# Hourglass attention into a quick-GELU MoE: scores on 64 partitions from batch 2 on, and a re-ordered start

## The chip, the cores and the metric

The kernel runs on one core of one Trainium2 chip. The metric is the device time of the whole kernel in microseconds, the median of several runs; lower is better. The engines have these short names in the profile: PE (TensorE matmul), PEld (TensorE weight load), DVE (VectorE), ACT (ScalarE), POOL (GpSimd, here "Pool") and SP (SyncE, which here only issues DMAs). PSUM is the memory that TensorE writes; SBUF holds everything else.

## The reference

Attention over 8 batches, 8 heads, 576 tokens and a head size of 64, in two parts that are added: a local part, in which each token sees the tokens less than 4 away, and a part in which q, k and v are first averaged over groups of 4 tokens (144 groups) and the result is repeated 4 times. The sum, 4608 tokens by 512, goes through a feed-forward layer of width 2048.

```python
    q_d = q.reshape(B, H, Sd, factor, D).mean(axis=3)        # k_d, v_d alike
    out_d = sm_attn(q_d, k_d, v_d)
    out_up = np.repeat(out_d, factor, axis=2)
    mask = np.abs(pos[:, None] - pos[None, :]) < factor
    scores = np.where(mask, scale * np.matmul(q, k.transpose(0, 1, 3, 2)), -1e9)
    out_local = np.matmul(softmax(scores), v)
    x = out_up + out_local                                   # to 4608 x 512
    h = x @ w_in
    return (h * (1.0 / (1.0 + np.exp(-1.702 * h)))) @ w_out
```

## The kernel before

The order of instructions on each engine is the order in which the code is written; no scheduler moves them. The feed-forward part runs in 9 groups of 512 tokens (the loop from L800). In a group, `mm1` makes 16 blocks of 4 matmuls (L616) into the two PSUM banks `PM`, each followed by the activation on ACT (L627), and `mm2` makes 4 output tiles of 16 matmuls (L672), which ACT scales (L657) and SP stores (L662). Group g carries the attention of batch b = g + 1 with it: `attention` returns seven steps, and `POS` (L701) says ahead of which block or matmul each is put (group 0: `POS_0`). With `POS`, steps 13 (`s_pe(0)`: scores of heads 0 to 3), 16 (`s_act(0)`: exp and mask) and 33 (`s1`: both for heads 4 to 7), 42 and 53 (`avn`: probabilities times v, for pairs of heads 0, 1 and then 2, 3), 62 and 71 (`tr`: transposing back and writing x). A number of 16 or more stands in `mm2`, at that number less 16.

Ahead of the blocks of a group stands the preparation of its batch (L818 to L831):

- `prep_qk` (L266) lets DVE transpose k and q of 4 heads (L260). A head's 64 dimensions come to lie as 32 partitions times a pair `a` of neighbouring elements, so the four heads fill the 128 partitions.
- `pool_qk` (L270) adds 4 tokens to one on Pool, in two additions (L276, L285), into `kdT` and `qdT`.
- `load_qk` issues four loads of the next batch's k and q on Pool's queue (L194); `prep_v` (L289) casts v on Pool; `load_v` (L214) issues ten loads of the next batch's v on SP; `prep_v4` (L293) adds 4 tokens of `v4` to one in six additions on Pool (L297, L300) into `vd`. `load_v4` (L223) loads `v4` with six DMAs on SP, for b over 2 at the start of the batch's own group, behind the last store of the group before.

`scores` (L340) multiplies in tiles of 32 rows by 64 columns: 5 blocks of tokens, two halves `a`, two sides `par` and four heads make 80 matmuls (L351), the two halves accumulating. `scores_d` (L362) does the same with the averaged q and k, 24 matmuls (L369). `av_local` (L402, matmuls at L408) and `av_down` (L416, L430) multiply with v; `av_down` is the first reader of `vd`, in three parts, one for each third of the 144 groups. `normalise` divides on DVE (L441, L443), `transp` and `merge` (L449, L546) bring x into `xT`.

PSUM is three double banks `PA` for attention and two banks `PM` for the feed-forward part.

The start, ahead of the loop (L710 to L794), does batch 0's attention alone. Loads wait at two gates, which are tiny copies that read one tile and write another, so that the load behind must wait: w_in's gate at L728 (Pool waits for a piece of v 0), and v 1's load, whose gate L708 is a copy on DVE that waits for w_out's first load. w_out's second half waits on Pool (L808) for v 1. Batch 0's averaged scores of heads 4 to 7 go into `PA[1]` (L757), between the first and the second pair of heads; their exp on ACT frees that bank for the second pair. `turned` (L776) transposes a pair of heads and copies the result to `xT` (`copy_x`, four copies on ACT); `part` starts the first feed-forward blocks as the pieces of x come.

Of the kernel before, what the change touches and what calls it, by code (L numbers as in the profile page):

```python
# [8 lines left out]
FP32 = mybir.dt.float32  # L9
BF16 = mybir.dt.bfloat16  # L10
AF = mybir.ActivationFunctionType
ALU = mybir.AluOpType
# [7 lines left out]
def kernel(  # L20
# [18 lines left out]
    inv_sqrt_d = 1.0 / math.sqrt(D)  # L39
    KSTART = (0, 56)  # L40
    QSTART = (0, 60)

    ctx.enter_context(
        tc.manual_schedule(engines={ET.PE, ET.Activation, ET.DVE, ET.Pool, ET.SP})
# [19 lines left out]
    eds = [persist.tile([128, 2, 464], BF16, name=f"ed{i}") for i in range(2)]  # L64
    v4 = persist.tile([128, 3, HP, 4 * D], FP32, name="v4")
    kdT = [persist.tile([128, 160, 2], BF16, name=f"kdT{i}") for i in range(NQ)]

    PA = [psum.tile([128, 2, 512], FP32, name=f"pa{i}") for i in range(3)]
    PM = [psum.tile([128, 512], FP32, name=f"pm{i}") for i in range(2)]
# [51 lines left out]
    def fill():  # L121
        nc.vector.memset(wz, 0.0)
        for t in kdT:
            nc.vector.memset(t[:, SD:160, :], 0.0)
        for t in vbs:
            nc.vector.memset(t[:, :, :, 64:65], 1.0)
        for t in vds:
            nc.vector.memset(t[:, :, :, 64:65], 4.0)
        for t in es:
            nc.vector.memset(t[:, :, 300:304], 1.0)  # L130
        for t in eds:
            nc.vector.memset(t[:, :, 432:464], 1.0)
# [122 lines left out]

    def prep_1(name, b, qd):
        store, dst = {"k": (kf, kT), "q": (qf, qT)}[name]
        tt = work.tile([128, S, 2], BF16, name=f"{name}T{qd}", tag=f"{name}T{qd}", bufs=1)
        t32 = tt.rearrange("p t a -> p (t a)").bitcast(FP32)
        nc.vector.transpose(  # L260
            out=t32.rearrange("p (i c) -> p c i", c=18),
            in_=store[b, qd].bitcast(FP32).rearrange("p (c d) -> p c d", c=18),
        )
        dst[b, qd] = tt

    def prep_qk(b, qd):  # L266
        prep_1("k", b, qd)
# [2 lines left out]
    def pool_qk(b, qd, names="kq"):  # L270
        for name, src in (("k", kT), ("q", qT)):
            if name not in names:
                continue
            sv = src[b, qd].rearrange("p (j f) a -> p j f a", f=4)
            t1 = work.tile([128, SD, 2, 2], FP32, name="pq", tag="pq")
            nc.gpsimd.tensor_tensor(  # L276
                out=t1, in0=sv[:, :, 0:2, :], in1=sv[:, :, 2:4, :], op=ALU.add
            )
            if name == "k":
                dst = kdT[qd][:, 0:SD, :]  # L280
            else:
                t = work.tile([128, SD, 2], BF16, name=f"qdT{qd}", tag=f"qdT{qd}", bufs=1)
                qdT[b, qd] = t
                dst = t
            nc.gpsimd.tensor_tensor(  # L285
                out=dst, in0=t1[:, :, 0, :], in1=t1[:, :, 1, :], op=ALU.add
            )
# [51 lines left out]

    def scores(b, qd, barred=False):  # L340
        sp = [ps_tile(), ps_tile()]
        if barred:
            bar_others(sp)
        for i in range(5):
# [16 lines left out]

    def scores_d(b, qd, sd=None):  # L362
        sd = sd or ps_tile()
        for kc in range(3):
            for a in range(2):
                for r in range(4):
                    rows = slice(32 * r, 32 * r + 32)
                    j = r % 2
                    nc.tensor.matmul(  # L369
                        sd[64 * j : 64 * j + 64, r // 2, SD * kc : SD * kc + SD],  # L370
                        lhsT=kdT[qd][rows, 48 * kc : 48 * kc + 64, a],
                        rhs=qdT[b, qd][rows, :, a],
                        start=(a == 0), stop=(a == 1),
# [143 lines left out]
    def copy_x(b, hp, x):  # L517
        t0 = b * S
        for par in range(2):
            nc.scalar.copy(  # L520
                out=sub(xT[hp], t0 + 3 + 57 * par, (114, 5), (1, 57)),
                in_=sub(x[par], 3 - 3 * par, (57, 5), (1, 57)),
            )
            nc.scalar.copy(
                out=sub(xT[hp], t0 + 573 * par, (1, 3)),
                in_=sub(x[par], 285 * par, (1, 3)),
            )
# [173 lines left out]
    POS = [13, 16, 33, 42, 53, 62, 71]  # L701
    POS_0 = [16, 18, 27, 54, 68, 60, 76]
    VDP_0 = 52

    o, y, x = {}, {}, {}

# [18 lines left out]
    sp = scores(0, 0, barred=True)  # L725
    exp_local(0, sp)
    prep_qk(0, 1)
    nc.gpsimd.tensor_copy(out=w_in_bf[0:1, 0, 0:1], in_=vf[0][0:1, 1, 0, 0:1])  # L728
    load_w_in(0, 512)
    pool_qk(0, 1)  # L730
    load_w_in(512, 512)
    load_w_in(1024, 1024)
    for qd in range(NQ):
# [16 lines left out]
        prep_v(0, nc.vector, i=slice(i, i + 1))  # L750
    warm(6)
    prep_vd_pe(0, PA[2])
    o[0] = PA[0]
    av_local(0, 0, o[0])
    av_down(0, 0, o[0])
    y[0] = normalise(o[0])
    sd = scores_d(0, 1, PA[1])  # L757
    exp_down(1, sd)
    nc.scalar.preload_act_table_set("silu_and_others")
    for hp in range(1, 3):  # L760
        o[hp] = PA[hp]
        av_local(0, hp, o[hp])
        av_down(0, hp, o[hp])
        y[hp] = normalise(o[hp])
    warm(1)

    gT0 = new_gT()
    acc = PM + [PA[n][:, u, :] for n in (1, 2, 0) for u in range(2)]
# [31 lines left out]
    for g in range(n_groups):  # L800
# [15 lines left out]
                load_qk(2, qd)  # L816
            loads_2()
        elif b < B:  # L818
            if b > 2:
                load_v4(b)  # L820
            prep_qk(b, 0)
            pool_qk(b, 0)
            if b + 1 < B:
                for qd in range(NQ):
                    load_qk(b + 1, qd)
            prep_v(b, nc.gpsimd)
            if b + 1 < B:
                load_v(b + 1)
            prep_qk(b, 1)
            pool_qk(b, 1)  # L830
            prep_v4(b, nc.gpsimd)  # L831
        steps = {}
        if b < B:
            for n, f in zip(POS if g else POS_0, attention(b, None if g else (1, 2))):
                steps.setdefault(n, []).append(f)
            if g == 0:
                steps.setdefault(VDP_0, []).append(lambda: prep_vd_pe(1, PA[2]))
        gT = new_gT() if g else gT0
# [32 lines left out]
```

The softmax here doesn't subtract the row's maximum and nothing guards it: scores larger than these inputs give would overflow.

## Time and profile before

| What | us |
|---|---|
| median of 11 runs | 333.92 (331.88 to 335.98) |
| the profiled execution, its own time | 333.1 |
| span of that execution in the profile | 331.3 |
| L616, 528 matmuls of `mm1` into PM: busy | 120.2 |
| L672, 493 matmuls of `mm2` into PM: busy | 114.1 |
| L351, 1280 matmuls of `scores`: busy | 14.0 |
| L369, 384 matmuls of `scores_d`: busy | 9.7 |
| L260, 32 transposes on DVE, 1.24 to 1.25 each: busy | 39.9 |
| L276 and L285, 64 additions on Pool: busy | 58.4 |
| L297 and L300, 36 additions on Pool: busy | 36.5 |
| Pool's idle time that a transpose of k ended | 104.4 |

Times are of one execution, counted from the span's start. A matmul's busy time is that of all matmuls of the line together, since they overlap; the mean of a single one (some 200 ns for the small ones) is longer than its share. A line of the timeline gives start, length, engine, code line, what is written from what, and in brackets the idle time before it with what ended it. The chain of waits is followed back from the last instruction: at each moment it names the work that the end waited for, and "issue" is time for which the profile shows no reason. SPq is time in which SP issues a DMA. The DMA share of a window is the mean busy share of 16 DMA engines and can go a little over 1, as packets overlap.

### The profile page before, as it was taken

The numbers are of one execution on the slowest core, as the hardware profiler recorded it, in microseconds if no ns is written. First come the engines' busy times: TensorE is split into PE (matmuls) and PEld (weight loads), VectorE is DVE, ScalarE is ACT, GpSimd is POOL, SyncE is SP. The second block draws the span as 40 slices with busy tenths as digits, with TensorE's granted clock in tenths as the row PEclk, the third lists the DMA queues.
The fourth block names the chain that finished last, engine by engine and source line by source line (L and its number), as shares of the span: only waits on it lengthen the run. The fifth ranks groups of instructions, "written<-read, shape, count | busy, mean of one in ns | idle before, by whom it ended". The sixth has DMA issues, their size and how long they took to land.

```text
span 331.3 us, 11215 instructions
## 1 busy us (share of the span) xinstructions
PE 309.1 (93%) x4986; PEld 159.5 (48%) x5043; DVE 132.1 (40%) x213; ACT 184.5 (56%) x323; POOL 138.3 (42%) x168
## 2 busy tenths in 40 slices
PE   8657999889999999999999999998999999999995
PEld 3445455545554455445544554445444544444444
DVE  4757302690367127712672167316740570000000
ACT  2543585366836774667467745675466647425611
POOL 7791734029802990199019900991099000000000
PEclk9977999999999999999999999999999999999999
DMA  7999979999913992299329921993180110011011
GB/s 126 184 177 211 180 139 189 192 230 199 190 55 100 205 199 76 89 190 192 108 75 211 205 90 67 203 197 102 45 176 2 44 57 32 2 64 63 2 60 66
DMA packets 63552, 41.36 MB, mean 125 GB/s; under 512 B 44048, under 2 KB 54416, under 8 KB 63504
## 3 DMA queue, kind: packets, MB, share of 16 engines
q1 hardware_dynamic: 55056, 26.95, 35.1%
q0 software_dynamic: 8304, 13.63, 23.6%
q8 instruction: 39, 0.64, 0.9%
q14 instruction: 9, 0.07, 0.1%
q10 hardware_dynamic: 144, 0.07, 0.1%
HBM read 44.83 MB, written 9.44 MB: 164 GB/s over the span
## 4 chain that ended last, share of the span: by engine, by line
PE 87%; issue 4%; SPq 3%; DVE 2%; DMA 2%; ACT 1%; DVEq 0%; ACTq 0%
PE pm L616 35%; PE pm L672 33%; SPq L214 3%; PE pa L351 3%; PE pa L616 2%; PE pa L430 2%; PE pa L408 2%; PE pa L369 2%; PE pa L457 2%; DMA vf<-in_v_dram 2%; PE pa L672 1%; PE pm L687 1%; DVE y L443 1%; PE pa L483 1%; ACT vd L321 0%
## 5 line engine op out<-in xcount | busy, mean ns | idle before, releaser
L616 PE MATMUL pm<-xT,w_in_bf 128*128 128x512 bf16 x528 | 120.2, 380 | 1.2 <-DVE xT L559 0.5
L672 PE MATMUL pm<-w_out_bf,gT 128*128 128x512 bf16 x493 | 114.1, 379 | 5.4 <-issue 5.2
L627 ACT ACTIVATE gT<-pm 128x512 bf16<-128x512 f32 x136 | 81.0, 598 | 44.6 <-PE pm L616 44.6
L616 PEld LDWEIGHTS <-w_in_bf 128*128 128x128 bf16 x576 | 55.8, 98 | 68.0 <-issue 2.0
L672 PEld LDWEIGHTS <-gT 128*128 128x128 bf16 x560 | 51.8, 98 | 59.5 <-issue 0.2
L276 POOL TENSOR_TENSOR pq<-kT 128x576 f32<-128x576 bf16 x16 | 18.6, 1160 | 104.4 <-DVE kT L260 104.4
L394 DVE TENSOR_TENSOR es<-es,mask 128x600 bf16<-128x600 bf16 x28 | 20.5, 750 | 94.7 <-ACT es L380 94.0
L657 ACT ACTIVATE osb<-pm 128x512 f32<-128x512 f32 (+2 forms) x35 | 20.8, 594 | 40.2 <-PE pm L672 35.9
L532 ACT COPY od<-pa 128x384 f32<-128x384 f32 (+1 forms) x56 | 18.4, 412 | 30.8 <-DVE y L443 22.4
L443 DVE TENSOR_TENSOR y<-pa,rc 128x896 bf16<-128x896 f32 x32 | 34.9, 1092 | 1.1
L553 DVE TENSOR_TENSOR xT<-pa,od 128x570 bf16<-128x570 f32 x28 | 21.1, 754 | 10.4 <-ACT od L532 10.3
L380 ACT ACTIVATE es<-pa 128x600 bf16<-128x600 f32 x32 | 19.8, 668 | 7.4 <-PE pa L351 7.1
L297 POOL TENSOR_TENSOR v<-v 112x512 f32<-112x512 f32 x18 | 22.8, 1264 | 0.0
L659 DVE TENSOR_SCALAR osb<-pm 128x128 f32<-128x128 f32 x1 | 0.3, 292 | 55.3 <-ACT osb L657 55.3
L260 DVE STREAM_TRANSPOSE kT<-kb 128x576 f32<-128x576 f32 x16 | 20.0, 1251 | 3.9 <-DMA kb<-in_k_dram 3.8
L260 DVE STREAM_TRANSPOSE qT<-qb 128x576 f32<-128x576 f32 x16 | 19.9, 1242 | 1.6 <-DMA qb<-in_q_dram 1.5
L276 POOL TENSOR_TENSOR pq<-qT 128x576 f32<-128x576 bf16 x16 | 18.3, 1145 | 0.0
L291 POOL CAST vb<-vf 128x2560 bf16<-128x2560 f32 (+1 forms) x11 | 17.3, 1601 | 0.0
L441 DVE RECIPROCAL rc<-pa 128x14 f32<-128x14 f32 x32 | 7.7, 241 | 23.6 <-PE pa L430 23.6
L351 PE MATMUL pa<-qT,kT 32*64 32x60 bf16 x1280 | 14.0, 203 | 1.8 <-issue 1.4
L351 PEld LDWEIGHTS <-kT 32*64 32x64 bf16 x1280 | 11.9, 104 | 7.0 <-issue 5.7
L386 ACT ACTIVATE ed<-pa 128x864 bf16<-128x864 f32 x16 | 14.4, 897 | 1.5 <-PE pa L369 1.5
(86 smaller groups left out, 251.7 us busy)
## 6 DMA issues: line engine op xcount, KB each, us to landing
vf<-in_v_dram SPq DMA_DIRECT2D x80, 128.0 KB, 5.1
out_dram<-osb SPq DMA_DIRECT2D x35, 256.0 KB, 2.0
v<-in_v_dram SPq DMA_DIRECT2D x36, 192.0 KB, 5.1
kb<-in_k_dram POOLq DMA_DIRECT2D x16, 288.0 KB, 6.5
qb<-in_q_dram POOLq DMA_DIRECT2D x16, 288.0 KB, 7.5
w_out_bf<-in_moe_w_out_dram POOLq DMA_DIRECT2D x4, 512.0 KB, 12.4
w_in_bf<-in_moe_w_in_dram POOLq DMA_DIRECT2D x2, 512.0 KB, 5.7
w_in_bf<-in_moe_w_in_dram POOLq DMA_DIRECT2D x1, 1024.0 KB, 11.2
```

Source lines behind the costliest of these rows:

```text
L260: nc.vector.transpose(out=t32.rearrange("p (i c) -> p c i", c=18), in_=store[b, qd].bitcast(FP32).rearrange("p (c d) -> p c d", c=18),)
L276: nc.gpsimd.tensor_tensor(out=t1, in0=sv[:, :, 0:2, :], in1=sv[:, :, 2:4, :], op=ALU.add)
L297: eng.tensor_tensor(out=t1[0:112], in0=x[:, :, 0:2, :], in1=x[:, :, 2:4, :], op=ALU.add)
L351: nc.tensor.matmul(sp[r // 2][64 * par : 64 * par + 64, r % 2, 60 * i : 60 * i + 60], lhsT=kT[b, qd][rows, k0 : k0 + 64, a], rhs=qT[b, qd] ...
L380: nc.scalar.activation(out=es[2 * qd + u][:, :, 0:300], in_=sp[u][:, :, 0:300], func=AF.Exp, scale=inv_sqrt_d,)
L394: nc.vector.tensor_tensor(out=ev, in0=ev, in1=mask, op=ALU.mult)
L443: nc.vector.tensor_tensor(out=y, in0=ov[:, :, :, 0:D], in1=rc.to_broadcast([128, 2, 7, D]), op=ALU.mult,)
L553: eng.tensor_tensor(out=sub(xT[hp], t0 + 3, (57, 2), (114, 5), (1, 57)), in0=sub(x, 3, (509, 2), (57, 5), (1, 57)), in1=sub(od, 3, (57, 2) ...
L616: nc.tensor.matmul(acc, lhsT=w_in_bf[:, dmc, ffc * 128 : (ffc + 1) * 128], rhs=xT[dmc][:, g * TG : g * TG + TG], start=(dmc == 0), stop=(d ...
L627: nc.scalar.activation(out=gT[:, ffc, :], in_=acc, func=AF.Silu, scale=GELU_SCALE)
L657: eng.activation(out=osb, in_=ap, func=AF.Copy, scale=1.0 / GELU_SCALE)
L672: nc.tensor.matmul(ops[t], lhsT=gT[:, ffc, t * 128 : (t + 1) * 128], rhs=w_out_bf[:, ffc, :], start=(ffc == 0), stop=(ffc == n_ffc - 1),)
```

## The change

Four edits stand in it.

1. In the start, the gate of w_in waits for v 0's third chunk instead of its second, and Pool adds k of heads 4 to 7 ahead of that gate instead of behind it (q stays behind).
2. The averaged scores of batch 0's heads 4 to 7 go to the two `PM` banks, with an exp for each bank; `av_local` of the first two pairs stands ahead of `av_down` of both, and the third pair comes after the exps.
3. `copy_x` of the last pair takes DVE for the half `par` = 1. In DVE's order these two copies stand ahead of batch 1's four transposes.
4. From batch 2 on a head's k and q lie on 64 partitions. The transpose is made twice into a tile with two halves `x`; then, for each half and each of two groups of 64 partitions, a DMA on SP copies the 32 partitions of one head, shifted by one element, over the 32 partitions of the other. So the even elements lie on 32 partitions and the odd ones on the next 32, in slot 0 of each pair; half `x` holds heads 2r + x. Scores are then made by 40 matmuls of 64 rows instead of 80 of 32, averaged scores by 12 instead of 24, with nothing to accumulate. Pool's additions work on slot 0 alone, with as many elements as before, and `pq` has one buffer instead of two. For k and q of 4 heads each that makes 16 copies a batch on SP. `prep_qk(b, 1)` moves ahead of `load_v(b + 1)`, so that its copies stand ahead of those loads on SP, and `load_v4(b + 1)` becomes a step at 34 of the group before, from batch 3 on.

```diff
@@ prep_1
+        n = 2 if b >= ROWS64 else 1
+        tt = work.tile([128, 2, S, 2], BF16, name=f"{name}T{qd}", tag=f"{name}T{qd}", bufs=1)
+        for x in range(n):
+            t32 = tt[:, x].rearrange("p t a -> p (t a)").bitcast(FP32)
+            nc.vector.transpose(
+                out=t32.rearrange("p (i c) -> p c i", c=18),
+                in_=store[b, qd].bitcast(FP32).rearrange("p (c d) -> p c d", c=18),
+            )
+        if n == 2:
+            for x in range(2):
+                f = tt[:, x].rearrange("p t a -> p (t a)")
+                for r in range(2):
+                    src = 64 * r + 32 * x
+                    to = 64 * r + 32 * (1 - x)
+                    nc.sync.dma_start(
+                        out=f[to : to + 32, 0 : 2 * S - 1], in_=f[src : src + 32, 1 : 2 * S]
+                    )
@@ pool_qk
+            if b >= ROWS64:
+                sv = src[b, qd].rearrange("p x (j f) a -> p (x j) f a", f=4)[:, :, :, 0]
+                t1 = work.tile([128, 2 * SD, 2], FP32, name="pq", tag="pq", bufs=1)
+                nc.gpsimd.tensor_tensor(
+                    out=t1, in0=sv[:, :, 0:2], in1=sv[:, :, 2:4], op=ALU.add
+                )
...
@@ scores
+        if b >= ROWS64:
+            for j in range(2):
+                for i in range(5):
+                    for par in range(2):
+                        for u in range(2):
+                            rows = slice(64 * u, 64 * u + 64)
...
+                            nc.tensor.matmul(
+                                sp[u][64 * par : 64 * par + 64, j, 60 * i : 60 * i + 60],
+                                lhsT=kT[b, qd][rows, j, k0 : k0 + 64, 0],
+                                rhs=qT[b, qd][rows, j, q0 : q0 + 60, 0],
+                                start=True, stop=True,
+                                tile_position=(64 * u, 64 * par),
+                            )
+            return sp
@@ copy_x
-            nc.scalar.copy(
+            cp = nc.vector.tensor_copy if par and hp == HP - 1 else nc.scalar.copy
+            cp(
@@ the start
-    nc.gpsimd.tensor_copy(out=w_in_bf[0:1, 0, 0:1], in_=vf[0][0:1, 1, 0, 0:1])
+    pool_qk(0, 1, "k")
+    nc.gpsimd.tensor_copy(out=w_in_bf[0:1, 0, 0:1], in_=vf[0][0:1, 2, 0, 0:1])
     load_w_in(0, 512)
-    pool_qk(0, 1)
+    pool_qk(0, 1, "q")
...
-    o[0] = PA[0]
-    av_local(0, 0, o[0])
-    av_down(0, 0, o[0])
-    y[0] = normalise(o[0])
-    sd = scores_d(0, 1, PA[1])
-    exp_down(1, sd)
-    nc.scalar.preload_act_table_set("silu_and_others")
-    for hp in range(1, 3):
+    for hp in range(2):
         o[hp] = PA[hp]
         av_local(0, hp, o[hp])
+    for hp in range(2):
         av_down(0, hp, o[hp])
         y[hp] = normalise(o[hp])
+    scores_d(0, 1, PM)
+    for u in range(2):
+        nc.scalar.activation(
+            out=eds[1][:, u, 0:432], in_=PM[u][:, 0:432],
+            func=AF.Exp, scale=inv_sqrt_d / 16.0,
+        )
+    nc.scalar.preload_act_table_set("silu_and_others")
     warm(1)
+    o[2] = av(0, 2, 2)
+    y[2] = normalise(o[2])
@@ the loop
-            if b > 2:
-                load_v4(b)
             prep_qk(b, 0)
             pool_qk(b, 0)
...
             prep_v(b, nc.gpsimd)
+            prep_qk(b, 1)
             if b + 1 < B:
                 load_v(b + 1)
-            prep_qk(b, 1)
             pool_qk(b, 1)
...
+            if g and b + 1 < B:
+                steps.setdefault(V4, []).append(lambda b=b: load_v4(b + 1))
```

## The prediction

> **What bounds the kernel now.** I read the page's busy times and its chain first, then the chain of waits in order of time, then each engine's timeline in one batch's period (104 to 138 us) and in the stretch before batch 2 (37 to 75 us), and last the landing times of transfers.
>
> ```profile
> PE 309.1 (93%) x4986; PEld 159.5 (48%) x5043; DVE 132.1 (40%) x213; ACT 184.5 (56%) x323; POOL 138.3 (42%) x168
> PE 87%; issue 4%; SPq 3%; DVE 2%; DMA 2%; ACT 1%; DVEq 0%; ACTq 0%
> ```
>
> TensorE is the chain. From 47 us on it hardly waits, so a gain must shorten its own work, and a loss comes from anything that arrives late. The chain from 91 to 131 us (start, length, what) shows batch 2's and batch 3's attention between MoE matmuls:
>
> ```profile
> 92.72 0.12 PE pa L430 x13
> 92.84 0.26 issue
> 93.10 0.23 PE pa L430 x5
> ...
> 115.48 0.77 PE pa L351 x79
> 116.25 0.39 PE pa L369 x23
> ...
> 126.28 0.28 PE pa L408 x20
> 126.56 0.15 PE pa L430 x17
> ```
>
> A scores call costs 0.77 us and the down-scores 0.39 to 0.46. L430 is the first reader of `vd`, the last product of Pool's work for a batch. How much room does Pool leave? The timelines of VectorE and Pool in that period:
>
> ```profile
> 104.56 1.26 DVE L260 STREAM_TRANSPOSE kT<-kb 128x576 f32<-128x576 f32 x1
> 107.83 1.24 DVE L260 STREAM_TRANSPOSE qT<-qb 128x576 f32<-128x576 f32 x1
> 105.90 1.15 POOL L276 TENSOR_TENSOR pq<-kT 128x576 f32<-128x576 bf16 x1 [15.82 <-DVE kT L260]
> 108.97 0.66 POOL L285 TENSOR_TENSOR qdT<-pq 128x288 bf16<-128x288 f32 x1
> 123.12 0.84 POOL L300 TENSOR_TENSOR vd<-v 112x256 bf16<-112x256 f32 x1
> ```
>
> Call T0 the start of a batch's first transpose (104.56). Pool starts at T0+1.34, runs without a pause and ends at 123.96 = T0+19.4. TensorE's ninth L430 matmul, the first that needs the last third of `vd`, comes at about 126.65 = T0+22.1. **Pool's slack is 2.7 us a batch**: this is the number on which the change turns. Before batch 2 the queues are tight in another way:
>
> ```profile
> 37.58 0.14 DVE L708 CAST vf<-w_out_bf 1x1 f32<-1x1 bf16 x1 [1.27 <-DMA w_out_bf<-in_moe_w_out_dram]
> 37.85 14.70 SPq L214 DMA_DIRECT2D vf<-in_v_dram  x12
> 65.95 4.41 SPq L226 DMA_DIRECT2D v<-in_v_dram  x6
> 70.46 2.46 SPq L662 DMA_DIRECT2D out_dram<-osb  x4
> ```
>
> v 1's load starts when VectorE's gate (L708) has run; v 2, v4 2 and group 0's four stores then stand on SP one behind another until 72.9. The DMA engines are full in most of that stretch (share 1.10 in window 48:64, 1.07 in 67:76), so a later start there is not made up.
>
> [...] stores of 256 KB take 2.0 us median from issue to landing, and 1.5 us is the least for any store (64 KB). [...] So halving the matmuls does not halve the time: the trace has 80 of the first in 0.77 us (9.6 ns each), 20 of the second (L408) in 0.28 us (14 ns each). [...] I keep L276's and L285's durations; no run here shows these forms. [...] Here the granted clock is 0.66 in window 20:30, where TensorE is sparse.
>
> **The change, part by part.**
>
> *Prologue.* Pool adds k of heads 4 to 7 before w_in's gate, and the gate waits one chunk longer (13.5 for 12.2). Behind it on Pool stand w_in's first load (12.73, now some 13.9; first read at 30.1, far off), q's additions (end 17.6, now about 16.5) and the later loads, all a little earlier. v 0's last chunk, which landed at 19.6, should come about 1 us sooner, though VectorE's constants end at 18.4 and its three v casts take 0.5 us each, so I count 0.5. Down-scores in PM no longer hold PA[1]: before, pair 1's L408 stood until 23.75 (1.0 us of it waiting for ACT's exp); now it follows pair 0's at once, beside the vd copy. Two exps of 432 columns replace one of 864 (0.89 us), some 0.15 more. Together turned(0) starts about 1.2 us sooner (0 to 2). The 1.7 us pause at 28.16 ("issue", an instruction fetch ends just before) has the same instructions ahead of it and moves along. The split copy of the last x is off the path: ACT ended it at 36.08 and its first reader came at 37.3.
>
> *What the split copy does to VectorE.* Its two copies (0.4+0.2 us estimated from ACT's 0.42 and 0.19) stand ahead of batch 1's four transposes. Those ran from 30.84 as k and q landed; now they wait for turned(3), over at 35.2-1.2 = 34.0. They then run 34.6 to 39.1 (3x1.09+1.26), the gate follows at 39.2, and v 1's load starts at 39.5 instead of 37.85: **+1.6 us** (+0.8 to +2.8 for a prologue gain of 2 to 0). w_out's last half is needed at 56.9 and landed by 52.4, so it survives; v 2, v4 2 and the stores move by +1.6.
>
> *64-row scores, the gain.* 40 matmuls at 14 ns make 0.56, so 0.21 us less for each of 12 calls. The down-scores stream as many columns per row group as before (6x144), so nothing is gained; bounds for both 0 to 0.35. About 0.4 us a batch.
>
> *64-row scores, the price.* VectorE makes eight transposes instead of four (idle there until 121.99, so hidden by itself). SP issues 16 copies of 32x2302 bytes (72 KB) a batch, each about 0.33 us (the stores' L662 figure). A copy from SBUF to SBUF is not in the trace: bounds 1.3 us (a bit under the 64 KB store) to 2.5 us; I take 1.5 from issue. q's last transpose ends at T0+4.51, its second copy is issued at T0+4.9, landed T0+6.45; Pool's two additions take 1.85, so qdT is ready at T0+8.35 where it was at T0+5.02. Behind it in Pool's order stand four k/q loads, the v cast, the second half's additions and v4's sums: 14.4 us. The end is T0+22.75, with 0.1 for `pq`'s single buffer T0+22.85, against 22.1 wanted in the old timing. The scores' saving is swallowed by the wait. **+0.75 us for each of batches 3 to 6, +3.0** (0.4 to 1.5 each). Batch 7 has no loads on Pool (2.1 us less) and keeps its gain: -0.4. v4's load at step 34 takes six issues out of SP's way at T0, and is hidden behind later stores; the copies stand ahead of the next v load, which has 10 us of room.
>
> *Batch 2.* Here the copies stand behind v4 2 and four stores. [...] The stores' packets end at 77.1, landing 77.6; q's fourth copy then lands at 79.1, +1.6 is 80.7, Pool's additions end at 82.6, and 14.4 later is 97.0. TensorE wanted it at 92.8, with a pause of 0.26 right after that now lies within the wait: **+3.9 us** in absolute time (2.2 to 6.0). The prologue's gain is lost in it. Shorter waits fall in scores and down-scores first; the last one, some 3 us, might cost clock (0 to 1.7; I take 0).
>
> **Sum.** 3.9+3.0-0.4 = +6.5 us. The profiled execution took 333.1 us (span 331.3), so 339.6; it lies 0.8 below the median of 333.92, on which the forecast stands: **340.4 us**. Its own range is 338 to 344.
>
> **Rivals.** *Hidden copies (faster).* If qdT is late by less than Pool's slack, the end is TensorE's own: 12x0.2 from scores and 1.2 from the prologue, -3.6, 330.3 us. The mechanism is the 64-row array with all preparation under cover; it decides where the extra delay (3.3 by my sum) stays under 2.7 less 0.4 earlier need, so under 2.3 us, and where batch 2's copies pass SP's jam. For it: VectorE, SP and DMA all idle for long after T0. Against: two more transposes cost 2.2 alone. *Only batch 2 waits.* Pool's new forms or the copies are quicker by 1 us: 3.9-5x0.4 = +1.9, 335.8. *Slow copies.* Rows starting on an odd element may move badly[...]: 2.7 us more in each of six batches, +16, 350. For it: nothing measured excludes it; against: each row is one run of 2302 bytes, as k's rows of 2304 are.
>
> **Chances.** Forecast 0.62, hidden 0.17, only batch 2 0.13, slow copies 0.08. About 0.5% (1.7 us) is what a measurement tells from no change. Slower 0.77, within 0.06 (part of "only batch 2"), faster 0.17. The range, 332 to 346, leaves out most of "hidden" and "slow copies".
>
> **What would show it.** Right: L430 waiting for Pool (`vd`) in batches 2 to 6, most in batch 2; periods near 34.1 instead of 33.4 us for batches 3 to 6; batch 1's transposes after 34 us and v 1's load near 39.5; L351's 80 matmuls replaced by 40 in 0.5 to 0.6 us. Wrong: copies landing in under 1 us, Pool's additions shorter than 1.85 us a pair, SP free at T0 of batch 2, or no idle before L430.

## The result, and the profile after

The changed kernel takes 365.67 us (median of 12 runs, 364.0 to 370.78); the kernel before, on the same chip, 334.4 us (47 runs, 331.63 to 337.54). The ratio is 1.0954, with a 95% interval from 1.0926 to 1.0982: 31 us slower, where the prediction had 6.5. Ratios here and below leave out executions that took over 1.5% more than the fastest of the same kernel, so a ratio can differ a little from the quotient of two medians. The profiled execution took 364.8 us, with a span of 363.0 us; it was 331.3 us before.

The page of the changed kernel first: its busy times, the shares of the chain that ended last, and the last two columns of its DMA issues (KB each, median us from issue to landing).

```profile
PE 315.1 (87%) x4363; PEld 157.1 (43%) x4419; DVE 160.8 (44%) x241; ACT 183.8 (51%) x322; POOL 141.6 (39%) x168
...
PE 41%; DVE 17%; POOL 15%; DMA 11%; issue 7%; SPq 5%; ACT 3%; DVEq 1%; POOLq 0%; ACTq 0%
...
kT<-kT SPq DMA_DIRECT2D x48, 71.9 KB, 2.1
qT<-qT SPq DMA_DIRECT2D x48, 71.9 KB, 2.1
```

TensorE does some 600 instructions less and is busy 6 us longer. Its share of the chain fell from 87% to 41%; transposes, copies and Pool's additions are now in it. The view of waits says for what TensorE stands (us in total, times, longest):

```profile
PE pa L491 <- POOL vd L331: 19.3, 11, 2.0
PE pa L416 <- POOL qdT L301: 6.1, 4, 2.3
```

L491 is `av_down`, the reader of `vd` that was L430 before, and these 19.3 us are the greater part of the loss. Its source is to be found on SP and Pool. Batch 3 is the example: its first transpose starts at 113.48, which is its T0. SP's timeline, with the 16 copies in groups of four:

```profile
114.80 2.49 SPq L276 DMA_DIRECT2D kT<-kT  x4
117.38 2.44 SPq L276 DMA_DIRECT2D qT<-qT  x4
119.93 2.43 SPq L276 DMA_DIRECT2D kT<-kT  x4
122.46 2.45 SPq L276 DMA_DIRECT2D qT<-qT  x4
```

A copy holds SP for 0.58 us in the median, and four take 2.5 to 2.6 us with the gaps. SP thus needs 10.1 us for the 16, while VectorE's eight transposes are over at T0+8.8: from the second group on it is SP that sets the pace. Pool's timeline of the same batch:

```profile
118.89 1.15 POOL L292 TENSOR_TENSOR pq<-kT 128x576 f32<-128x576 bf16 x1 [18.86 <-DMA kT<-kT]
...
121.48 1.15 POOL L292 TENSOR_TENSOR pq<-qT 128x576 f32<-128x576 bf16 x1 [0.70 <-DMA qT<-qT]
...
123.31 0.57 POOL L198 DMA_DIRECT2D kb<-in_k_dram  x1
...
130.54 1.15 POOL L292 TENSOR_TENSOR pq<-qT 128x576 f32<-128x576 bf16 x1 [0.89 <-DMA qT<-qT]
...
138.23 0.73 POOL L331 TENSOR_TENSOR vd<-v 112x256 bf16<-112x256 f32 x1
```

Pool begins at T0+5.4 (T0+1.34 before) and ends at 138.96, which is T0+25.5 (T0+19.4 before; T0+25.5 to T0+25.9 in batches 3 to 6). Note the second q wait, at 130.54. The chain of waits has the last q copy in it:

```profile
124.32 6.07 DMA qT<-qT
```

It landed 6.1 us after its issue and not 2.0, while the four k/q loads that Pool issued from 123.31 on were on the same DMA engines; e5_loads_later below takes these loads away, and there the longest landing is 3.9 us. TensorE's timeline shows what the late end of Pool's chain does:

```profile
131.14 0.52 PE L381 MATMUL pa<-qT,kT 64*64 64x60 bf16 x40
132.59 0.38 PE L416 MATMUL pa<-qdT,kdP 64*64 64x144 bf16 x12 [0.93 <-ACT es L441]
...
135.14 0.20 PE L491 MATMUL pa<-vd,ed 48*64 48x65 bf16 x4
136.99 0.22 PE L491 MATMUL pa<-vd,ed 48*64 48x65 bf16 x4 [1.65 <-POOL vd L331]
139.01 0.38 PE L491 MATMUL pa<-vd,ed 48*64 48x65 bf16 x10 [1.80 <-POOL vd L331]
...
140.38 3.23 PE L734 MATMUL pm<-w_out_bf,gT 128*128 128x512 bf16 x10 [0.34 <-issue]
```

The 40 scores matmuls take 0.52 us where 80 took 0.77: that gain is there. But `av_down` stands twice, 1.65 and 1.80 us, for two thirds of `vd` in turn. The ninth of its matmuls comes at 139.01, T0+25.5, against T0+22.0 before. And the ten MoE matmuls after it take 3.23 us, where ten take 2.3 at full clock: the granted clock is 0.50 from 138.8 to 142.2. The lateness is handed on: VectorE transposes a batch right behind its last additions into x of the batch before (the last one ends at 113.37, T0 is 113.48), so T0 itself moves and no batch makes the delay good. The windows from one T0 to the next, batch 2 to batch 6, carry both losses (length; busy time and number of instructions of PE, PEld, DVE, ACT and POOL; granted clock, DMA share, GB/s):

```profile
69.46:113.48 44.02, 35.74 (x490) 17.10 (x497) 20.61 (x30) 20.82 (x36) 17.96 (x19) 0.92 0.79 179
113.48:152.18 38.70, 33.25 (x491) 16.64 (x497) 21.66 (x29) 20.86 (x37) 17.93 (x19) 0.96 0.72 154
152.18:189.85 37.67, 31.96 (x491) 16.06 (x497) 20.61 (x28) 20.95 (x37) 17.86 (x19) 1.00 0.69 159
189.85:229.70 39.85, 34.20 (x491) 16.84 (x497) 21.29 (x28) 20.95 (x37) 17.92 (x19) 0.91 0.69 150
229.70:268.31 38.61, 33.18 (x491) 16.61 (x497) 21.61 (x29) 20.85 (x37) 18.10 (x19) 0.96 0.70 154
```

Before, these periods were 33.88, 33.39, 33.52, 33.62 and 34.29 us, all at a clock of 1.00. Batch 4 before, for the third row:

```profile
137.95:171.47 33.52, 32.62 (x595) 16.88 (x601) 16.33 (x25) 20.95 (x37) 17.52 (x19) 1.00 0.68 144
```

The third row lost nothing to the clock and is still 4.15 us longer: that is the lateness alone. For the others (1 - clock) x length is 1.5 to 3.6 us each, 10.2 us over the five, but this is too much: TensorE stood in part of the slow time, and batch 2's first slow stretch (84.2 to 87.6) only shortened a wait behind it. Counted from the ninth `av_down` matmul to the first matmul of the next pair, batch 4 needs 3.07 us at full clock and batches 2, 3, 5 and 6 need 4.76, 4.53, 5.49 and 4.46 us: 7.0 us more together.

Batch 2 lost most, for the reason that its queue shows:

```profile
67.53 4.14 SPq L230 DMA_DIRECT2D v<-in_v_dram  x6
71.78 2.27 SPq L724 DMA_DIRECT2D out_dram<-osb  x4
74.15 2.63 SPq L276 DMA_DIRECT2D kT<-kT  x4
```

T0 is 69.46 there, but the first copy is issued 4.7 us later, behind v4 2 and group 0's stores; Pool's chain ends at T0+30.6. TensorE also waits for `qdT` there, 2.26 us at one time.

The growth of the span, 31.7 us, by its parts:

| part | predicted | measured |
|---|---|---|
| start, to T0 of batch 2 (69.46 for 70.68) | contained in the next | -1.2 |
| batch 2 | +3.9, the start's gain within it | +10.1 |
| batches 3 to 6 | +3.0 | +5.3 +4.2 +6.2 +4.3 = +20.0 |
| batch 7 to the end (94.69 for 91.92) | -0.4 | +2.8 |

### The profile page after: what moved, and what is told of

Read it like the earlier page. It is cut to its first block, busy times and chain, and to the rows that moved or that the text cites. A ratio compares the mean times of both kernels' runs of the same rounds, so it can differ in the third digit from the quotient of the medians.

```text
span 363.0 us, 10241 instructions
## 1 busy us (share of the span) xinstructions
PE 315.1 (87%) x4363; PEld 157.1 (43%) x4419; DVE 160.8 (44%) x241; ACT 183.8 (51%) x322; POOL 141.6 (39%) x168
## 4 chain that ended last, share of the span: by engine, by line
PE 41%; DVE 17%; POOL 15%; DMA 11%; issue 7%; SPq 5%; ACT 3%; DVEq 1%; POOLq 0%; ACTq 0%
PE pm L734 16%; PE pm L678 12%; DMA qT<-qT 9%; POOL v L328 7%; SPq L276 5%; DVE xT L615 5%; DVE qT L266 4%; DVE kT L266 4%; POOL vd L331 4%; DVE y L504 3%; POOL pq L292 3%; PE pa L678 2%; PE pa L491 2%; DMA qb<-in_q_dram 2%; ACT od L594 2%
## 5 line engine op out<-in xcount | busy, mean ns | idle before, releaser
L734 PE MATMUL pm<-w_out_bf,gT 128*128 128x512 bf16 x493 | 121.1, 396 | 5.9 <-issue 5.8
L678 PE MATMUL pm<-xT,w_in_bf 128*128 128x512 bf16 x528 | 122.5, 384 | 1.4 <-DVE xT L621 0.7
L292 POOL TENSOR_TENSOR pq<-kT 128x576 f32<-128x576 bf16 x12 | 13.9, 1161 | 117.8 <-DMA kT<-kT 80.2
L455 DVE TENSOR_TENSOR es<-es,mask 128x600 bf16<-128x600 bf16 x28 | 24.5, 893 | 68.2 <-ACT es L441 67.5
L266 DVE STREAM_TRANSPOSE kT<-kb 128x576 f32<-128x576 f32 x28 | 32.9, 1243 | 2.5 <-DMA kb<-in_k_dram 1.9
L266 DVE STREAM_TRANSPOSE qT<-qb 128x576 f32<-128x576 f32 x28 | 32.8, 1238 | 0.8 <-DMA qb<-in_q_dram 0.8
L491 PE MATMUL pa<-vd,ed 48*64 48x65 bf16 x640 | 14.6, 202 | 19.5 <-POOL vd L331 19.3
L491 PEld LDWEIGHTS <-ed 48*64 48x64 bf16 x640 | 11.3, 112 | 20.9 <-issue 20.8
L292 POOL TENSOR_TENSOR pq<-qT 128x576 f32<-128x576 bf16 x12 | 14.1, 1176 | 9.4 <-DMA qT<-qT 8.1
L331 POOL TENSOR_TENSOR vd<-v 112x256 bf16<-112x256 f32 x18 | 13.9, 770 | 1.4
```

The source lines that it names most:

```text
L266: nc.vector.transpose(out=t32.rearrange("p (i c) -> p c i", c=18), in_=store[b, qd].bitcast(FP32).rearrange("p (c d) -> p c d", c=18),)
L292: nc.gpsimd.tensor_tensor(out=t1, in0=sv[:, :, 0:2], in1=sv[:, :, 2:4], op=ALU.add)
L331: eng.tensor_tensor(out=vds[b % 2][0:112, kc, :, 0:D], in0=t1[0:112, :, 0, :], in1=t1[0:112, :, 1, :], op=ALU.add,)
L455: nc.vector.tensor_tensor(out=ev, in0=ev, in1=mask, op=ALU.mult)
L491: nc.tensor.matmul(o[64 * pos : 64 * pos + 64, j, c0 : c0 + 65], lhsT=Ed[64 * j : 64 * j + 48, u, q0 : q0 + 64], rhs=vd[64 * j : 64 * j + ...
L678: nc.tensor.matmul(acc, lhsT=w_in_bf[:, dmc, ffc * 128 : (ffc + 1) * 128], rhs=xT[dmc][:, g * TG : g * TG + TG], start=(dmc == 0), stop=(d ...
```

## The experiments

Theory A: the loss is the 64-row preparation alone. The copies end Pool's chain late, `av_down` waits for `vd`, and the half clock adds to it. The rivals: B, the new order of loads or the edits of the start; C, the double transposes and Pool's strided forms; D, the 64-row matmuls themselves.

### One part alone: e1_start, e2_rows

The start's edits without any 64-row batch:

```diff
-    ROWS64 = 2
+    ROWS64 = 8
```

> Everything of the change but the 64-row scores: w_in's gate, the down-scores in PM, the split copy of the last x, and the new places of the k/q and v4 loads; no batch uses 64 rows, so there is no second transpose and no copy. Theory A (the loss is the 64-row preparation alone: it ends Pool's chain 6 us late in every batch, TensorE waits for vd and then runs at half clock for about 3.4 us): 332 to 333 us, ratio 0.995, the start some 1.5 us earlier, no wait of L491 on Pool over 0.3 us. Theory B (the later k/q and v4 loads or VectorE's split copy carry a good part): 338 to 350 us. Theory D (the 64-row matmuls themselves run badly or hold PSUM): as A, 333.

333.74 us against 334.07 for the kernel before; ratio 0.997, interval 0.9935 to 1.0006. It is slightly above theory A's 332 to 333. B falls: the start, the later loads and VectorE's split copy together cost nothing that can be measured, and the start's gain can hardly be measured either. What each of them does alone is not told apart here.

Then the other part alone: the 64-row scores on the start of the kernel before (gate, down-scores in PA[1] and ScalarE's copies as they were).

> The 64-row scores alone (double transposes, copies, Pool's new forms, new load order), on the start of the kernel before. Theory A: the whole loss is here and the start's 1.5 us are missing: 366 to 368 us, periods of 38 to 40 us for batches 3 to 6, 44 for batch 2. Theory B: 345 to 355.

365.6 us, ratio 1.0893 (1.0817 to 1.0968): all of the loss, just under the 366 to 368 expected. Batch 2's period is 38.92 us here, not 44: its T0 comes at 72.36, when SP is done with the stores (72.88), and its first copy is issued at 73.69, 1.3 us after T0. So in these two executions what the start's edits win ahead of batch 2, its copies give back behind v4 2 and the stores.

### Without the copies: e3_nocopy

```diff
-                    nc.sync.dma_start(
-                        out=f[to : to + 32, 0 : 2 * S - 1], in_=f[src : src + 32, 1 : 2 * S]
-                    )
```

> The changed kernel without the 16 copies a batch: the odd elements are not put in place, so the scores of batches 2 to 7 are computed from the wrong elements; every other instruction stays, the double transposes too. Theory A: Pool starts as soon as the transposes are there; first half's qdT at T0+6.9, end of vd about T0+20.8, earlier than TensorE wants it (T0+21.5), no wait, no half clock: 330 to 332 us. Theory C (the double transposes or Pool's strided forms cost as much as the copies): waits of 1 us and more remain in each batch, 340 to 350. Theory D (the 64-row matmuls themselves): 355 or more, since all of them are still there.

328.48 us, ratio 0.9832 (0.9776 to 0.9889). C and D fall: eight transposes, Pool's new forms and all the 64-row matmuls are still there, and this is 5.6 us faster than before, better than the 330 to 332 of theory A. Two of its periods (batch 4 and 5, columns as above):

```profile
136.15:169.02 32.87, 32.87 (x500) 15.99 (x499) 21.35 (x29) 21.11 (x37) 17.93 (x19) 1.00 0.67 146
169.02:201.90 32.88, 32.66 (x498) 15.89 (x497) 22.11 (x29) 20.85 (x37) 17.93 (x19) 1.00 0.70 146
```

These two are 32.9 us for 33.5 and 33.6; all five from batch 2 to 6 are 166.41 us for 168.70, so some 0.5 us a batch is what the half as many matmuls are worth, which fits two scores calls of 0.52 us for 0.77 each. Pool's chain ends at T0+21.3 and the ninth `av_down` comes at T0+21.4: even with no copy at all, Pool's slack is used up to the last 0.1 us. Of its 2.5 to 2.7 us the second transposes take 1.5 (qdT of the first half at T0+6.5 for T0+5.1), Pool's slower operations behind that 0.4, and TensorE, which now comes earlier, 0.6; the copies had nothing left to hide in.

### What `vd` waits behind: e4_vfirst

```diff
         elif b < B:
+            if b > 2:
+                prep_v(b, nc.gpsimd)
+                prep_v4(b, nc.gpsimd)
             prep_qk(b, 0)
```

(and the same two calls left out further down for those batches)

> The changed kernel with all copies, but from batch 3 on Pool does the v cast and v4's sums ahead of the k/q additions of the batch, so that what L491 waits for no longer stands behind the copies; batch 2 as in the changed kernel. Theory A: vd ends about T0+8, L491 waits for nothing in batches 3 to 7; the second half's down-scores now come last on Pool, about T0+27, and TensorE wants them near T0+14.5 of the old timing plus the wait, so if they are late the wait moves to the down-scores rather than going away: 338 to 345 us if they are in time for the most part, 355 to 365 if the wait only moves. Theory D: 365, unchanged.

342.62 us, ratio 1.0207 (1.0137 to 1.0277): 23 of the 31 us are gone, with every copy still made. TensorE's timeline in batch 3 (T0 is 113.34):

```profile
132.88 0.38 PE L416 MATMUL pa<-qdT,kdP 64*64 64x144 bf16 x12 [1.36 <-POOL qdT L301]
...
135.43 0.32 PE L491 MATMUL pa<-vd,ed 48*64 48x65 bf16 x17
```

`av_down` waits for nothing. The second half's down-scores still wait for Pool, for 1.36 us, and the granted clock stays at 1.00 behind it. Batches 3 to 6 take 33.2 to 34.8 us; batch 2, left in the old order, still takes 43.75.

### The size of single terms: e5_loads_later, e6_warm, e7_from3, e8_even

The k/q loads of the next batch, moved on Pool from ahead of the v cast to behind the second half's additions:

```diff
             pool_qk(b, 0)
-            if b + 1 < B:
-                for qd in range(NQ):
-                    load_qk(b + 1, qd)
             prep_v(b, nc.gpsimd)
...
             pool_qk(b, 1)
+            if b + 1 < B:
+                for qd in range(NQ):
+                    load_qk(b + 1, qd)
             prep_v4(b, nc.gpsimd)
```

> The changed kernel with the next batch's four k/q loads moved on Pool's queue from ahead of the v cast to behind the second half's q additions. Theory A1 (the loads cost Pool's chain twice: 2.1 us of Pool's time ahead of vd, and their packets stand ahead of the last two q copies on the DMA engines, so these land 6 us instead of 2 us after issue and Pool waits 0.9 us more): chain end about T0+22.6 instead of T0+25.6, a wait of some 1 us in batches 3 to 6 and no half clock after it; 342 to 348 us. Theory A2 (the last copies are slow by themselves): their landing stays at 6 us, chain end T0+23.5, 350 to 355 us.

362.54 us, ratio 1.0838 (1.0754 to 1.0921): neither, and only 3 us less than the changed kernel. (The profiled execution, at 367.51 us, is the longest of its four; what is read from it here are landings and Pool's chain.) What A1 says of the landing is right, as the query of the copies' line shows (6.3 us was the longest in the changed kernel):

```profile
DMA to landing us min/median/max: 2.0/2.1/3.9
```

But Pool's chain ends at T0+24.6 to T0+25.2, hardly earlier, and the expectation itself was wrong there: behind the q additions the loads still stand ahead of v4's sums, so their 2.1 us of Pool's time stayed in the chain. `av_down` waits for `vd` 19.4 us in all, as in the changed kernel (19.3).

Then seven matmuls of zeros ahead of each of the two blocks of `av_down` that wait (`other` is the MoE bank that is not being summed):

```diff
             for kc, x, c2 in blocks:
+                if b >= ROWS64 and hp == 0 and kc and x == c2 == 0:
+                    for _ in range(7):
+                        nc.tensor.matmul(
+                            other, lhsT=wz[:, 0:128], rhs=wz, start=True, stop=True
+                        )
```

> The changed kernel with seven matmuls of zeros (128x512, 1.5 us together) ahead of each of the two av_down blocks that wait for vd, from batch 2 on, into the MoE bank that is free then. Theory A (after each wait TensorE runs at half clock for some 3.4 us, which costs about 1.8 us a batch beyond the wait itself): the end of Pool's chain stays at T0+25.5, the granted clock stays at 1.0 there, and 7 to 11 us come back: 355 to 359 us. Rival (the matmuls behind the wait are slow for another reason, such as PSUM evictions or weights): 365 to 368.

358.75 us, ratio 1.0728 (1.0656 to 1.08): 6.9 us less than the changed kernel, at the upper edge of what theory A expected. The timeline of batch 4 (T0 is 151.24):

```profile
175.33 1.69 PE L487 MATMUL pm<-wz 128*128 128x512 bf16 x7
177.20 0.28 PE L497 MATMUL pa<-vd,ed 48*64 48x65 bf16 x10 [0.18 <-POOL vd L331]
...
177.79 2.55 PE L740 MATMUL pm<-w_out_bf,gT 128*128 128x512 bf16 x11
```

`vd` is as late as ever (the ninth matmul at T0+25.96), but the zeros keep TensorE at work, the clock stays at 1.00 in batches 3 to 6, and the MoE matmuls run at their 0.23 us. The half clock is thus a cost of its own, about 7 us of the 31 by this run. The count in the changed kernel's trace gave 7.0 us for batches 2 to 6, and gives 1.7 more for batch 7 in the same way (4.76 for 3.07); e6 has three pauses of 0.8 to 1.0 us of its own, in which nothing is shown to be waited for.

Batch 2 without 64 rows:

```diff
-    ROWS64 = 2
+    ROWS64 = 3
```

> The changed kernel with the 64-row scores from batch 3 on, batch 2 as before. Theory A (batch 2's copies stand on SP behind v4 2's load and group 0's stores, and that batch alone costs some 9 us): period from batch 2 to 3 back at 34.5 us, 355 to 358 us. Rival (batch 2 costs no more than the others): 360 to 361.

361.7 us, ratio 1.0827 (1.0766 to 1.0887): only 4 us less, close to the rival's 360 to 361. Batch 2's period is back at 35.19 us, as theory A had it, but batches 3 to 6 are longer than in the changed kernel, 160.9 us together for 154.8. Two of them:

```profile
144.02:183.73 39.71, 35.35 (x498) 16.88 (x497) 21.62 (x29) 20.85 (x37) 18.19 (x19) 0.91 0.66 150
183.73:224.21 40.48, 35.68 (x498) 16.98 (x497) 20.61 (x29) 20.95 (x37) 18.00 (x19) 0.92 0.71 148
```

They have 6.8 us at a clock of 0.50 each, where batch 4 of the changed kernel had none, although `av_down` waits for 1.65 and 1.80 us in the second of them as in that batch 4. The changed kernel's trace shows when its clock falls: from batch 2 on at 84.18, 101.25, 138.80, 213.89, 254.85 and 292.40 us, which lie 5, 11, 22, 12 and 11 times 3.413 us apart, and it stays at 0.50 for 3.41 us or twice that. Three stretches of this length, on the same grid, one of batch 3 and two of batch 4:

```profile
135.39:138.80 3.41, 0.22 (x4) 0.11 (x4) 0.00 (x0) 0.00 (x0) 3.25 (x4) 1.00 0.87 188
172.93:176.34 3.41, 1.76 (x34) 0.78 (x33) 0.53 (x1) 1.39 (x2) 3.25 (x5) 1.00 0.81 182
176.34:179.76 3.42, 1.46 (x57) 1.05 (x57) 1.23 (x2) 0.00 (x0) 1.67 (x2) 1.00 0.85 218
```

In batch 3 both waits lie in one such stretch, in which TensorE works for 0.22 us, and in the next one the clock is 0.50. In batch 4 one stretch ends between the same two waits, TensorE works for 1.76 and 1.46 us in the two, and the clock stays at 1.00. But ahead of batch 5's fall TensorE worked for 1.65 us, so the work in a stretch does not settle it, and that the place of a wait on the grid decides is not shown: no run moved a wait against the grid.

The copies with both sides on an even element:

```diff
-                        out=f[to : to + 32, 0 : 2 * S - 1], in_=f[src : src + 32, 1 : 2 * S]
+                        out=f[to : to + 32, 0 : 2 * S], in_=f[src : src + 32, 0 : 2 * S]
```

> The changed kernel with its copies starting on an even element on both sides (2304 bytes a row instead of 2302, so the odd elements are not moved by one place and batches 2 to 7 use the wrong elements); everything else stays. Theory A (the cost of a copy is its issue on SP and its completion, not the odd start): issue 0.5 to 0.6 us and landing 2.0 us stay, 362 to 366 us. Rival of the prediction (rows that start on an odd element move badly): landing near 1.5 us, issue near 0.35 us, 345 to 355 us.

368.11 us, ratio 1.1019 (1.0943 to 1.1095), above both ranges; issue 0.58 us for kT's copies and landing 2.0 us in the median, as with the odd start (0.58 and 2.1). The prediction's "slow copies" came nearest in time, but the odd start is refuted as a reason here, and Pool's new forms are none either: its additions take 1.15 and 0.67 us in the changed kernel, 1.15 and 0.66 before. That they would keep those durations was the author's assumption.

### Towards a faster version: e9_last to e12_best

```diff
-    ROWS64 = 2
+    ROWS64 = 3
...
+            if b >= ROWS64:
+                prep_v(b, nc.gpsimd)
+                prep_v4(b, nc.gpsimd)
             prep_qk(b, 0)
             pool_qk(b, 0)
-            if b + 1 < B:
-                for qd in range(NQ):
-                    load_qk(b + 1, qd)
-            prep_v(b, nc.gpsimd)
+            if b < ROWS64:
+                prep_v(b, nc.gpsimd)
             prep_qk(b, 1)
...
             pool_qk(b, 1)
-            prep_v4(b, nc.gpsimd)
+            if b < ROWS64:
+                prep_v4(b, nc.gpsimd)
+            if b + 1 < B:
+                for qd in range(NQ):
+                    load_qk(b + 1, qd)
```

> Three moves at once on the changed kernel: 64-row scores from batch 3 on (batch 2 as before), Pool does the v cast and v4's sums ahead of the k/q additions in those batches, and the next batch's k/q loads come last on Pool in every batch, so that no load stands between the copies and Pool's additions. Theory A (the 64-row scores gain some 0.5 us a batch once nothing waits for Pool): second half's qdT ready near T0+16.5, before TensorE's second down-scores want it (about T0+17.5); no wait above 0.5 us on Pool, no half clock; 329 to 331 us. If the 32 copies' traffic or SP's pace costs something else (loads of k/q landing after the next transposes want them, for one), 333 to 337.

342.45 us, ratio 1.0231 (1.0191 to 1.0271): a miss, though Pool does what was wanted. The second half's qdT is ready at T0+15 to T0+16.2, and no wait for Pool of over 0.4 us is left among TensorE's. It stops all the same, once a batch. Batch 4 (T0 is 140.82):

```profile
161.71 0.33 PE L469 MATMUL pa<-vb,es 64*64 64x65 bf16 x17
164.68 0.19 PE L469 MATMUL pa<-vb,es 64*64 64x65 bf16 x1 [2.64 <-issue]
```

The DMA view of 161 to 165.5 (packets, MB, and share of the 16 engines for each queue):

```profile
q0 software_dynamic: 322, 0.63, 73.8%
q1 hardware_dynamic: 1339, 0.33, 38.5%
q8 instruction: 1, 0.02, 1.2%
```

The engines are full with k/q loads (q0, 73.8%) and v loads (q1, 38.5%), and one 16 KB transfer on queue 8, which the page lists as `instruction`, lies among them. It starts at 162.28 and takes 0.88 us; TensorE goes on 1.5 us after its end. In the five batches with such a pause (1.4 to 2.7 us) TensorE resumes 1.3 to 1.7 us after the end of such a transfer. The pages have 39 of these transfers at 10,029 matmuls and weight loads in the kernel before and 34 at 8,782 in the changed one, one for 257 and one for 258; that they bring TensorE's instructions is inferred from this.

Against e9_last, the last x copied by ScalarE:

```diff
-            cp = nc.vector.tensor_copy if par and hp == HP - 1 else nc.scalar.copy
+            cp = nc.scalar.copy
```

> As e9_last, with the last x of batch 0 copied by ScalarE alone, as in the kernel before. Theory A (VectorE's two copies only delay v 1's load by 1.4 us, which nothing waits for in the end): the same time as e9_last within 1 us, v 1's load near 37.5 us of the span. Rival (the split shortens the start): 1 to 2 us more than e9_last.

340.92 us, ratio 1.0204 (1.0163 to 1.0245). The interval overlaps with e9_last's, so the two are not told apart; v 1's load starts at 37.08 instead of 38.34. In the profiled executions batch 2's T0 is 65.59 here, 67.16 in e12_best with the same copies, and 69.00 in e9_last, so the split copy may cost the start something; one execution each does not show it.

Against e9_last, the k/q loads where the changed kernel has them:

```diff
             pool_qk(b, 0)
+            if b + 1 < B:
+                for qd in range(NQ):
+                    load_qk(b + 1, qd)
...
             pool_qk(b, 1)
-            if b + 1 < B:
-                for qd in range(NQ):
-                    load_qk(b + 1, qd)
```

> As e9_last, but with the k/q loads back in the place that they have in the changed kernel (on Pool behind the first half's q additions), for every batch. Reason for it: in e9_last TensorE no longer waits for Pool, but once a batch, 20 to 26 us after T0, it stands for 1.4 to 2.7 us with nothing that the profile shows, and starts again 1.3 to 1.7 us after the end of a 16 KB transfer on queue 8 (instructions), in a stretch where the DMA engines are full with k/q and v loads together. Theory E (the late loads hold up TensorE's instruction fetch): these pauses go; a wait of some 1.3 us for the second down-scores comes back in batches 3 to 7, 333 to 336 us. Rival (the pauses come from the instruction stream itself): pauses stay, 343 to 348.

335.81 us, ratio 1.0032 (1.0002 to 1.0063); the medians are 0.6% apart. It goes as theory E has it: the loads' place alone is worth 6.6 us. From batch 3 on one pause of that kind is left, 0.89 us, and it too ends 1.6 us after such a transfer; the second down-scores wait for Pool again, three times, 1.8 us at the longest. So this version, with its copies on SP, comes out at about the time of the kernel before.

Against e9_last, with ScalarE's copy as in e10_act (not shown again), later v loads, and the k/q loads between the second half's additions:

```diff
-    V4 = 34
+    V, V4 = 48, 66
...
-            if b + 1 < B:
-                load_v(b + 1)
-            pool_qk(b, 1)
+            pool_qk(b, 1, "k")
+            if ROWS64 <= b < B - 1:
+                for qd in range(NQ):
+                    load_qk(b + 1, qd)
+            pool_qk(b, 1, "q")
...
+                steps.setdefault(V, []).append(lambda b=b: load_v(b + 1))
                 steps.setdefault(V4, []).append(lambda b=b: load_v4(b + 1))
```

> A try at a version faster than both: as e9_last, with the next batch's k/q loads between the second half's k and q additions on Pool, the next v load at step 48 and the v4 load at step 66 (so that k/q and v loads no longer overlap), and the last x of batch 0 copied by ScalarE. Theory A with E: no wait on Pool above 0.5 us and no pause above 1 us: 329 to 332 us. If a v load is then late for Pool, or a fetch still stands behind loads: 334 to 342.

358.48 us, ratio 1.0739 (1.0684 to 1.0793): the worse of its two cases, and worse than that. With v and v4 loaded so late, the sums that now stand first on Pool run into the next batch (T0 is 140.33):

```profile
146.21 1.27 POOL L328 TENSOR_TENSOR v<-v 112x512 f32<-112x512 f32 x1 [0.81 <-DMA v<-in_v_dram]
...
152.32 1.14 POOL L292 TENSOR_TENSOR pq<-kT 128x576 f32<-128x576 bf16 x1
```

The first k addition starts at T0+12 instead of T0+5.4, and the down-scores wait 18.0 us in all. No version was found that beats the kernel before and still makes the copies; e3_nocopy shows that 5 to 6 us would be there if the odd elements came for nothing. Issuing the copies on another queue than SP's was not tried.

## Where the prediction was right, and why it was wrong

**Right: the place and the sign.** The prediction named Pool's slack of 2.7 us as the number on which the change turns, and L430 (now L491) waiting for `vd` as what would show it. The profile shows that, and e2, e3 and e4 establish the cause. The gain is also about as small as it was said to be: 0.4 us a batch predicted, some 0.5 in e3_nocopy. The predicted 14 ns a matmul came from L408's 64 by 64 tiles (20 in 0.28 us), against 9.6 ns for L351's 32 by 64 tiles (80 in 0.77 us); the new scores take 0.52 us for 40, 13 ns each, and the down-scores 0.38 us for 12 where 23 took 0.39.

**Right: the start.** T0 of batch 2 is 1.2 us earlier, the scores of batch 1 are 1.6 us earlier, batch 1's transposes run from 34.59, and v 1's load starts at 39.23, 1.4 us later than before (+1.6 predicted). That its gain is lost in batch 2 was right too. The pause at 28.16 before did not only move along: it is 3.36 us long for 1.7. Both end 1.3 to 1.4 us after a 16 KB transfer on queue 8 (at 28.43 before, at 26.03 after), like the pauses of e9_last.

**Wrong, the step that failed first: "SP issues 16 copies of 32x2302 bytes (72 KB) a batch, each about 0.33 us (the stores' L662 figure)", and "I take 1.5 from issue".** A copy holds SP 0.58 us (0.64 with its gap) and lands after 2.1 in the median. The stores had been taken as the price of a copy, though they go to another memory in another shape; the trace of before had SP busy for 0.43 us with a load of v4 and 0.64 us with a load of v in the median (L226, L214), so 0.33 was the smallest of three figures for that queue. Nor was the bound wide enough: the issue had no range at all, and the landing's 1.3 to 2.5 us left out the 6.1 of the last q copies. In batch 3 the error grows like this: q's last copy of the first half is issued at about T0+5.8 (T0+4.9 said), landing adds 2.0 (1.5 said), qdT is ready at T0+9.9 (T0+8.35 said), 1.5 us late.

**Wrong: the 14.4 us behind qdT.** They were taken as work without a pause. But the second half's copies take longest to land, with the four k/q loads issued in between on the same engines: Pool stands another 0.9 us, and its operations are a little longer (v4's first additions take 1.35 us in the mean for 1.26 before). So the chain ends at T0+25.5 to T0+25.9 and not at T0+22.85; against the T0+22.0 where `av_down` stood before, that is 3.5 to 3.9 us a batch in the place of 0.75. The prediction did look at the loads, but as time on Pool only.

**Wrong: "the last one, some 3 us, might cost clock (0 to 1.7; I take 0)".** This stood for batch 2 alone; for the other batches no cost of the clock was counted at all. (The 1.7 is what 3.41 us at a clock of 0.50 lose; the trace of before has one such stretch, from 30.60 to 34.01.) The lateness arrives in two waits of 1.65 and 1.80 us, with 0.22 us of work between them, and the clock is then 0.50 for 3.4 or 6.8 us in four of the five periods. That is 7.0 us by the count in the trace (8.7 with batch 7), and e6_warm, which keeps TensorE at work in the waits, came out 6.9 us faster.

**Wrong in size: batch 2.** The mechanism was right: the copies stand behind v4 2 and the stores, 4.7 us after T0. (That q's fourth copy would land 1.5 us after the stores was the author's estimate; the waits that the trace shows ahead of SP's copies name VectorE, 7.6 us, and TensorE, 0.2, and no transfer.) With the slower copies, the last of them behind other loads again, Pool ends at T0+30.6, and the batch takes 10.1 us more. e7_from3 brings that period back to 35.19 us, but only 4 us of it reach the end.

**Wrong: batch 7.** Without loads on Pool it was to keep its gain. Its chain ends at T0+22.9, `av_down` comes at T0+23.0 against T0+21.9 before, after one wait of 2.02 us, and 3.4 us of half clock follow: 1.1 and 1.7 us, together the 2.8 by which the stretch from its T0 to the end is longer.

**The rival "hidden" was further off than it looked.** It asked for an extra delay under 2.3 us; e3_nocopy has a chain that ends 1.9 us later with no copy made (T0+21.3 for T0+19.4), so some 0.4 us was left for all the copies.

The range was too narrow mainly because a tight slack turns every mis-sized term on the chain into time at full length, and here there were 16 copies of an unmeasured kind on it. The clock, which was put at nothing, added 7 to 9 us.

## What to carry to other kernels

Before a chain with little slack is given transfers, count them: issue time multiplied by number on the one queue, plus one landing, and allow for a longer landing where another queue issues loads meanwhile (6.1 us for 2.1 here). Where the slack is too small, ask what the waiting product itself needs: here `vd` needed none of the copies, and doing it first took back 23 of 31 us. And waits that lie close together, or a single one of 2 us, are to be priced with the clock that they can cost (1.4 to 2.4 us a batch here, in five batches of six).

## What the runs showed of the hardware

- A copy of 32 rows of 2302 bytes from SBUF to SBUF took 0.58 us of SP's queue and landed 2.1 us after issue in the median; issued while Pool's k/q loads were on the same engines it took 6.1 us, and 6.3 at the longest. Started on an even element (e8_even) it took 0.58 and 2.0 us.
- After waits of 1.65 and 1.80 us with 0.22 us of work between them the clock was 0.50 for 3.4 us in batch 3 and for 6.8 us in batch 5, and stayed at 1.00 in batch 4; one wait of 2.02 us (batch 7) was followed by 3.4 us of 0.50, and after one of 1.36 us in e4_vfirst the clock stayed at 1.00. In the changed kernel from batch 2 on the times at which the clock falls lie multiples of 3.413 us apart. From the ninth `av_down` matmul to the next pair, the same two waits were followed by 3.07 us in batch 4 and 5.49 us in batch 5.
- Transfers of 16 KB on queue 8, which the page lists as `instruction`, take the same DMA engines, one for 257 or 258 of TensorE's matmuls and weight loads. With k/q and v loads together in the attention's stretch (e9_last) TensorE stood 1.4 to 2.7 us a batch, and resumed 1.3 to 1.7 us after the end of such a transfer; moving the loads took 6.6 us off. In the view of waits this stands as "issue". That the loads delay the transfer is inferred from this; no run kept the loads and moved the transfers.
